# Transposing q and k of batches 4 to 7 with DMA crossbar transposes, loaded two batches ahead

## The chip, the cores and the metric

The kernel runs on one core of one Trainium2 chip. The metric is the time of one execution on the device in microseconds (us). Before the change the median of 14 runs is 361.16 us (360.59 to 365.67).

## What is computed

Eight batches of windowed attention with eight global positions, then a two-layer MLP with a snake activation over all 4608 tokens:

```python
scores = scale * np.matmul(q, k.transpose(0, 1, 3, 2))   # q, k, v: (8, 8, 576, 64), float32
mask = np.abs(pos[:, None] - pos[None, :]) <= 32
mask = mask | is_global[:, None] | is_global[None, :]    # 8 global positions
scores = np.where(mask, scores, -1000000000.0)
...                                                      # softmax over the last axis
x = attn_out.transpose(0, 2, 1, 3).reshape(4608, 512)
h = x @ w_in                                             # 512 -> 2048
s = np.sin(alpha * h)
g = h + s * s / (alpha + 1e-09)
out = g @ w_out                                          # 2048 -> 512
```

## The kernel before

The engines' names in the profile are PE (TensorE, the matmuls), ACT (ScalarE), DVE (VectorE), POOL (GpSimd) and SP (SyncE, which here only issues DMAs). Each engine runs its own instructions strictly in the order in which the program emits them, and waits in place for what an instruction needs.

**Stages.** The loop over `p` has nine stages. Stage p < 8 is the attention of batch p, interleaved with the second matmul of the MLP (`mm2`, L703) of token chunk p − 1, and then the first matmul of the MLP (`mm1`, L664) of chunk p with its activation. A chunk has 512 tokens, a batch 576. Stage 8 has MLP work only. The order within an attention is written out by hand: `attention(p, psA, at)` returns nine parts, steps j = −3 to 5, and after each part `run` emits some slots of `mm2` (`fill`) as further work for PE. A step j finishes unit j (`stage_V`), takes the denominator of unit j + 1 (`stage_D`), masks unit j + 2 (`stage_M`), runs what `at[j]` lists, and starts the scores of unit j + 3 (`stage_Q`). There are six units to a batch; each covers eight of the 48 (head pair, block of 48 query rows) pairs.

**Operands of the scores.** For each of the four head pairs hp, `kTw[hp]` holds the transposed keys in twelve overlapping windows of 112 rows, and `qT[hp]` the transposed queries; both also hold eight columns for the global positions. They are filled for batch p + 1 during the attention of batch p. `stage_T(b, hp)` does that with PE: `T_K` transposes K's 96-row pieces into the PSUM tile `Kps` (12 instructions, L456) and DVE copies the windows to `kTw` (L465); `T_Q` does the same for Q into the PSUM tile `qp`, and ACT copies that to `qT` (L643, after the scores of the step). For p > 1 the four head pairs stand at steps 2 to 5.

**Loads.** K, Q and V come from HBM in float32 and are converted to bfloat16 by DMAs that POOL issues. K and Q of a batch lie in the tiles `KS` and `QS` (pool `qkp`, two buffers each) with the sequence split into six pieces of 96 rows; `load_slots(b)` loads them in halves of the heads (`QUADS`: K, Q, K, Q; 288 KB each as stored, in runs of 64 elements, L128), then V in two halves and a small tail (L109, L115). In the attention of batch p these are the loads of batch p + 1, right after the first parts. `gather_kq(i)` (L259) fetches the global rows of K and Q for the batches 2i and 2i + 1. `globals_in` copies the columns of the global positions (L444, L448, on POOL).

**V.** `shift_v` (L143, L144) makes a second, shifted copy of V's windows from SBUF to SBUF, and `global_v` (L152) spreads the global rows of V; both are DMAs on SP's queue. SP's queue also carries the stores of the results from the tile `osb` (L715, two buffers).

**The end of an attention.** After the last unit, `stage_G` computes the rows of the global queries on DVE (`gs`, `xg`), and POOL writes them into `xT` with eight small copies (L588). `mm1` reads `xT`.

Of the kernel before, what the change touches and what calls it, by code (L numbers as in the profile page):

```python
# [17 lines left out]
def kernel(  # L18
# [11 lines left out]
    nc = tc.nc  # L30
    P = 128
    BF = DT.bfloat16
    F32 = DT.float32

    B, H, S, D = q.shape
# [3 lines left out]
    WIN = 32  # L39
# [4 lines left out]
    NHP = H // 2  # L44
    QB = 48
    KB = QB + 2 * WIN
    NW = S // QB
# [3 lines left out]
    TW = 96  # L51
    NTW = S // TW
# [7 lines left out]
    qkp = ctx.enter_context(tc.tile_pool(name="qkp", bufs=2))  # L60
# [16 lines left out]
    kTw = [const.tile([P, NW, P], BF, name=f"kTw{i}") for i in range(NHP)]  # L77
    qT = [const.tile([P, NW, QC], BF, name=f"qT{i}") for i in range(NHP)]
# [14 lines left out]
    qk = {}  # L93
# [8 lines left out]
    def v_loads(b, cuts):  # L102
        W = VW[b % 2]

        def even(h0, nh):
            Wf = W[:, 0, h0 : h0 + nh].rearrange("p h u d -> p (h u) d")
            n = nh * NU
            if b or h0:
                nc.gpsimd.dma_start(out=Wf[0:KB], in_=heads_ap(v, b, h0, -WIN, KB, 0, n))  # L109
            else:  # L110
                nc.gpsimd.dma_start(out=Wf[WIN:KB], in_=heads_ap(v, b, 0, 0, KB - WIN, 0, n))
                nc.gpsimd.dma_start(out=Wf[0:WIN, 1:n], in_=heads_ap(v, b, 0, -WIN, WIN, 1, n - 1))

        def tail():
            nc.gpsimd.dma_start(  # L115
                out=W[64 : KB - WIN, 1, :, NU - 1, :],
                in_=v[b, :, S - KB + WIN + 64 : S, :].rearrange("h p d -> p h d"),
            )

        return [partial(even, h0, nh) for h0, nh in cuts] + [tail]  # L120

    def kq_loads(b, cuts):
        QS = qkp.tile([TW, H, NTW, D], BF, name="QS")
        KS = qkp.tile([TW, H, NTW, D], BF, name="KS")
        qk[b] = (QS, KS)

        def rows(src, dst, h0, nh):
            nc.gpsimd.dma_start(  # L128
                out=dst[:, h0 : h0 + nh].rearrange("p h t d -> p (h t) d"),
                in_=heads_ap(src, b, h0, 0, TW, 0, nh * NTW),  # L130
            )

        return [partial(rows, s_, d_, h0, nh) for h0, nh in cuts for s_, d_ in ((k, KS), (q, QS))]
# [4 lines left out]
    def load_slots(b):  # L138
        return kq_loads(b, QUADS) + v_loads(b, QUADS)
# [18 lines left out]
    def w_load(dst, src):  # L158
# [23 lines left out]
        out=gall[:],  # L182
        in_=bass.AP(tensor=global_idx.tensor, offset=global_idx.offset, ap=[[0, P], [1, NG]]),
# [34 lines left out]
    def zero_v(i, eng=nc.vector):  # L218
# [5 lines left out]
        out=I8[:, 0:1], in0=I8[:, 0:1], scalar1=3, scalar2=None, op0=ALU.arith_shift_right  # L224
    )
    nc.vector.tensor_scalar(
        out=I8[:, 3:], in0=I8[:, 3:], scalar1=NG - 1, scalar2=None, op0=ALU.bitwise_and
    )
    nc.vector.tensor_scalar(
        out=I8[:, 1:2], in0=I8[:, 0:1], scalar1=2 * NHP, scalar2=None, op0=ALU.bitwise_and  # L230
    )
    nc.vector.tensor_scalar(
        out=identb[:], in0=Af[:], scalar1=0.0, scalar2=None, op0=ALU.is_equal
# [5 lines left out]
        out=Gsel[:, 1:2], in0=I8[:, 0:1], scalar1=2.0, scalar2=None, op0=ALU.mult  # L239
    )  # L240
    nc.vector.scalar_tensor_tensor(
        out=Gsel[:, 2:3], in0=I8[:, 1:2], scalar=1.0 / (2 * NHP) - 2.0, in1=Gsel[:, 1:2],
# [3 lines left out]
        out=Gsel[:, 3:], in0=I8[:, 3:], scalar=0.0, in1=Gf[:], op0=ALU.is_equal, op1=ALU.mult  # L246
    )
    nc.vector.tensor_reduce(
        out=Gsel[:, 0:1], in_=Gsel[:, 3:], axis=mybir.AxisListType.X, op=ALU.add
# [3 lines left out]
        out=rowi[:], in0=Gsel[:, 2:3], scalar=float(S), in1=Gsel[:, 0:1],  # L253
# [19 lines left out]
    def edges(t_):  # L273
# [13 lines left out]
        out=RF[:, 0:1], in0=Af[:, 0:1], scalar1=float(KB + NG - 1), scalar2=None, op0=ALU.is_le  # L287
    )
    nc.vector.scalar_tensor_tensor(
        out=RF[:, 1:2], in0=Af[:, 0:1], scalar=float(KB), in1=RF[:, 0:1],  # L290
# [3 lines left out]
        out=RF[:, 3:], in0=Af[:, 0:NG], scalar1=float(KB + 1), scalar2=None, op0=ALU.is_ge  # L294
    )
    nc.vector.tensor_tensor(
        out=OH[:], in0=T6[:, :, None].to_broadcast([P, NTW, NG]),
# [7 lines left out]
        out=EDGE[:, 0:1], in0=Af[:, 0:1], scalar1=float(WIN), scalar2=None, op0=ALU.is_ge  # L305
    )
    nc.vector.tensor_scalar(
        out=EDGE[:, 2:3], in0=Af[:, 0:1], scalar1=float(WIN + QB - 1), scalar2=None, op0=ALU.is_le
    )
    nc.vector.tensor_tensor(  # L310
        out=EDGE[:, 1:2], in0=EDGE[:, 0:1], in1=EDGE[:, 2:3], op=ALU.mult
    )
    nc.vector.tensor_scalar(
        out=MB[:, 0], in0=Af[:, 0:QB], scalar1=0.0, scalar2=None, op0=ALU.is_ge
    )
    nc.vector.scalar_tensor_tensor(
        out=MB[:, 1], in0=Af[:, 0:QB], scalar=float(2 * WIN), in1=MB[:, 0],
# [155 lines left out]
    def T_Q(b, hp, qpool, qtag, copy):  # L473
        Qps = qpool.tile([P, S], BF, name=qtag)
        T_half(qk[b][0], b, hp, Qps)
        return partial(copy, out=qT[hp][:, :, 0:QB], in_=Qps[:].rearrange("p (i c) -> p i c", c=QB))

    def stage_T(b, hp, pool, tag):
        T_K(b, hp, Kps, nc.vector.tensor_copy)
        return T_Q(b, hp, pool, tag, nc.scalar.copy)  # L480
# [267 lines left out]
    def with_extra(parts, extra, start, per):  # L748
        for i in range(start, len(parts)):
            k_ = (i - start) * per  # L750
            if extra[k_ : k_ + per]:
                parts[i] = partial(chain, parts[i], *extra[k_ : k_ + per])
        return extra[(len(parts) - start) * per :] if len(parts) > start else extra
# [58 lines left out]
    for p in range(NCH):  # L812
        fill = []
        if p == 0:
            phase_0()
            first.close()
        elif p < B:
            with phase_pool("psA", 1) as psA:
                for tag, shape, dt_ in (
                    ("den", [P, NB, QC], F32), ("Sp", [P, 2, CH], F32), ("num", [P, NB, QC], F32),  # L820
                    ("o2", [P, DM], F32), ("qp", [P, S], BF),
                ):
                    psA.tile(shape, dt_, name=tag)
                fill = mm2(p - 1, H2[p - 1], ((psC, "ops"), (psA, "o2")) * 2)
                if p == 1:
                    fill[:8] = [fill[i] for i in (0, 1, 4, 5, 2, 6, 3, 7)]
                T_ = lambda b, hp: partial(stage_T, b, hp, psA, "qp")
                if p == 1:
                    at = {-2: [T_(1, 2)], -1: [T_(1, 3)], 5: [T_(2, 0)]}
                elif p + 1 < B:  # L830
                    at = {2 + hp: [T_(p + 1, hp)] for hp in range(NHP)}
                else:
                    at = {}
                parts = attention(p, psA, at)
                counts = [1, 1, 1, 1, 1, 1, 2, 2, 4]
                fill.pop(0)()
                fill.pop(0)()
                if p + 1 < B:
                    with_extra(parts, load_slots(p + 1), 0, 4)
                    if p < 3:  # L840
                        parts[4] = partial(chain, parts[4], partial(gather_kq, p + 1))
                    for hp in range(NHP):
                        i_ = hp + LEAD + 1
                        parts[i_] = partial(chain, parts[i_], partial(globals_in, p + 1, hp))
                run(parts, counts, fill)
        else:
            fill = mm2(p - 1, H2[p - 1], ((psC, "ops"),) * 4)
        if p == 0:
            setup.release()
            spool = ctx.enter_context(tc.tile_pool(name="spool", bufs=4))  # L850
            osbp = ctx.enter_context(tc.tile_pool(name="osbp", bufs=2))
        with phase_pool("psB", 6) as psB:
            if p > 1:
                H2[p] = hpool.tile([P, NT, CH], BF, name="H2b")
            m1 = mm1(p, H2[p], psB, sq_last if p == B else sq_first if p == 0 else sq_late)
            if p < 3:
                m1[5] = partial(chain, m1[5], partial(globals_t, p + 1, psC, "ops"))
            if p + 1 < B:
                vs = [partial(shift_v, p + 1), partial(global_v, p + 1)]
                ts = {}  # L860
                if p == 0:
                    m1[5] = partial(chain, m1[5], *vs)
                    m1[6] = partial(chain, m1[6], w_loads[3])
                    ts = {12: (1, 0), 14: (1, 1)}
                else:
                    m1[10] = partial(chain, m1[10], *vs)
                    if p == 1:
                        ts = {2: (2, 1), 5: (2, 2), 8: (2, 3)}
                for i_, (b_, hp) in ts.items():
                    m1[i_] = partial(chain, m1[i_], partial(both, stage_T, b_, hp, psC, "ops"))  # L870
            run(m1, [1, 1, 1, 0] * (NT // 4) if p == B else [0] * NT, fill if p == B else [])
            if p == NCH - 1:
                for s in mm2(p, H2[p], ((psB, "hb"), (psC, "ops"), (psB, "hb"), (psB, "hb"), (psC, "ops")), cut=True):
                    s()
# [30 lines left out]
```

The softmax here doesn't subtract the row's maximum and nothing guards it: scores larger than these inputs give would overflow.

## Time and profile before

| | |
|---|---|
| median of 14 runs | 361.16 us (360.59 to 365.67) |
| the profiled execution | 361.23 us, of which the span from first to last instruction is 359.3 us |
| busy share of the span | PE 95%, ACT 68%, DVE 66%, POOL 57% |
| mean granted clock of PE | 0.962 |
| PE's share of the chain that ended last | 64% |
| DMA queue of POOL (software queue) | 123120 packets, 20.04 MB |

The profile shows one execution. Times in it are microseconds from the start of the span unless a column says ns. A line of a timeline or group names the source line, the engine, the operation, output and inputs, and the shapes; "x12" counts instructions; "[0.54 <-ACT qT L643]" is idle time of that engine before the instruction and what ended it. "issue" stands for a wait with no releaser that the profile shows. The chain that ended last follows the work back from the last instruction. Packets overlap on the 16 DMA engines, so that the DMA share can be over 1.

### The profile page before, as it was taken

To read this page: it belongs to the slowest core of one execution; us is meant where nothing else is said; L and a number is where in the kernel's file an instruction comes from. 1 tells how busy PE (TensorE), PEld (TensorE's weight loads), DVE (VectorE), ACT (ScalarE), POOL (GpSimd) and SP (SyncE) were. 2 spreads that over 40 slices of the span, in tenths; PEclk is the share of its full clock that TensorE was granted. 3 is DMA by queue.
4 is the path that set the end of the run, shared out by engine and by line. 5 is a ranking of instruction groups with operands and counts; after the bars stand their busy time and mean duration, and the time that the engine had idled before them with its cause. 6 is when DMAs were issued, how large, how long until landed. Compare 5 with 4: busy or idle time off the path is not lost.

```text
span 359.3 us, 9407 instructions
## 1 busy us (share of the span) xinstructions
PE 340.1 (95%) x3738; PEld 173.1 (48%) x3738; DVE 237.7 (66%) x527; ACT 245.8 (68%) x376; POOL 205.3 (57%) x302
## 2 busy tenths in 40 slices
PE   5589998899999999999999999999999999999996
PEld 5464445454445445544554445444544444444444
DVE  5666695648776687758774878487848864865610
ACT  3656786757886688758874888488858884844401
POOL 9857799245891589158905792479347205755000
PEclk9555999999999999999999999999999999999999
DMA  9999999932399409940994099419932001001012
GB/s 75 168 193 183 202 168 177 178 104 47 20 167 120 111 3 146 149 120 0 138 134 134 10 98 173 111 35 77 184 103 51 30 32 60 0 2 58 30 60 88
DMA packets 133149, 35.39 MB, mean 99 GB/s; under 512 B 121794, under 2 KB 126818, under 8 KB 133106
## 3 DMA queue, kind: packets, MB, share of 16 engines
q0 software_dynamic: 123120, 20.04, 78.1%
q1 hardware_dynamic: 9682, 14.63, 13.7%
q8 instruction: 29, 0.48, 0.5%
q10 hardware_dynamic: 304, 0.14, 0.1%
q14 instruction: 14, 0.11, 0.1%
HBM read 38.95 MB, written 9.44 MB: 135 GB/s over the span
## 4 chain that ended last, share of the span: by engine, by line
PE 64%; ACT 13%; DMA 9%; POOL 4%; DVE 4%; issue 4%; POOLq 1%; ACTq 0%; DVEq 0%
PE hb L664 28%; PE ops L703 12%; PE o L703 12%; DMA w_out<-in_moe_w_out_dram 4%; ACT E L507 3%; PE num L553 3%; PE Sp L501 3%; DMA VW<-in_v_dram 3%; DVE H2b L654 2%; PE den L535 2%; ACT L607 2%; DMA QS<-in_q_dram 2%; PE hb L703 2%; ACT Sb L671 2%; ACT L614 2%
## 5 line engine op out<-in xcount | busy, mean ns | idle before, releaser
L671 ACT ACTIVATE Sb<-hb,alphaT 128x512 bf16<-128x512 f32 x144 | 96.9, 684 | 58.2 <-PE hb L664 54.7
L664 PE MATMUL hb<-xT,w_in 128*128 128x512 bf16 x576 | 129.5, 380 | 0.2 <-DVE H2b L654 0.2
L681 POOL TENSOR_TENSOR S<-Sb 128x512 bf16<-128x512 bf16 x94 | 96.0, 1041 | 48.8 <-ACT Sb L671 45.4
L654 DVE SCALAR_TENSOR_TENSOR H2b<-S,recipT,hb 128x512 bf16<-128x512 bf16 x144 | 102.4, 741 | 30.7 <-POOL S L681 30.3
L664 PEld LDWEIGHTS <-w_in 128*128 128x128 bf16 x576 | 55.8, 98 | 67.3 <-issue 1.2
L703 PEld LDWEIGHTS <-H2b 128*128 128x128 bf16 x560 | 49.7, 98 | 56.2 <-issue 2.3
L703 PE MATMUL ops<-w_out,H2b 128*128 128x512 bf16 x304 | 73.9, 380 | 0.9 <-DMA w_out<-in_moe_w_out_dram 0.9
L703 PE MATMUL o<-w_out,H2b 128*128 128x512 bf16 x224 | 54.4, 381 | 0.0
L588 POOL COPY xT<-xg 128x4 bf16 x64 | 12.9, 201 | 67.9 <-DVE xg L586 64.4
L507 ACT ACTIVATE E<-Sp 128x896 bf16<-128x896 f32 x48 | 43.5, 906 | 8.5 <-PE Sp L501 5.2
L572 DVE TENSOR_TENSOR xT<-num,rec 128x384 bf16<-128x384 f32 (+1 forms) x60 | 26.0, 454 | 23.6 <-PE num L553 15.5
L541 ACT ACTIVATE lnd<-den 128x384 f32<-128x384 f32 x48 | 23.7, 493 | 18.8 <-PE den L535 18.2
L513 DVE TENSOR_TENSOR E<-E,MASK 128x896 bf16<-128x896 bf16 x48 | 30.1, 627 | 7.3 <-ACT E L507 7.3
L501 PE MATMUL Sp<-qT,kTw 64*128 64x56 bf16 x768 | 19.9, 189 | 8.0 <-ACT E L507 2.8
L553 PEld LDWEIGHTS <-VW 120*64 120x64 bf16 (+1 forms) x768 | 17.3, 117 | 19.6 <-issue 11.3
L543 ACT ACTIVATE rec<-lnd 128x384 f32<-128x384 f32 x48 | 25.1, 524 | 1.5
L501 PEld LDWEIGHTS <-kTw 64*128 64x128 bf16 x768 | 15.5, 96 | 19.7 <-issue 13.8
L465 DVE COPY kTw<-Kps 128x1344 bf16<-128x1344 bf16 x29 | 24.4, 840 | 0.0
L681 DVE TENSOR_TENSOR S<-Sb 128x512 bf16<-128x512 bf16 x34 | 17.6, 517 | 9.0 <-ACT Sb L671 8.9
L553 PE MATMUL num<-E,VW 120*64 120x56 bf16 (+1 forms) x720 | 20.6, 198 | 0.7 <-issue 0.7
L128 POOL DMA_DIRECT2D KS<-in_k_dram x18 | 20.7, 1150 | 0.6 <-issue 0.6
L535 PE MATMUL den<-E,ones 120*64 120x448 bf16 x96 | 18.9, 387 | 1.5 <-issue 0.8
(133 smaller groups left out, 308.2 us busy)
## 6 DMA issues: line engine op xcount, KB each, us to landing
out_dram<-osb SPq DMA_DIRECT2D x35, 256.0 KB
KS<-in_k_dram POOLq DMA_DIRECT2D x14, 288.0 KB
QS<-in_q_dram POOLq DMA_DIRECT2D x14, 288.0 KB, 17.2
VW<-in_v_dram POOLq DMA_DIRECT2D x12, 336.0 KB, 11.3
VW<-VW SPq DMA_DIRECT2D x7, 384.0 KB
w_in<-in_moe_w_in_dram POOLq DMA_DIRECT2D x2, 1024.0 KB
w_out<-in_moe_w_out_dram POOLq DMA_DIRECT2D x2, 1024.0 KB
VW<-VW SPq DMA_DIRECT2D x7, 240.0 KB
```

The lines of the kernel that those rows point to most:

```text
L501: nc.tensor.matmul(out=Sp[:, t, m * QC : (m + 1) * QC], lhsT=kTw[hp][pr, i, :], rhs=qT[hp][pr, i, :], start=True, stop=True, skip_group_ch ...
L507: nc.scalar.activation(out=E[:], in_=Sp[:, :, 0:EW], func=AF.Exp, scale=scale)
L513: nc.vector.tensor_tensor(out=E[:], in0=E[:], in1=mk[:, None, :].to_broadcast([P, 2, EW]), op=ALU.mult)
L535: nc.tensor.matmul(out=den[pr].rearrange("p u c -> p (u c)"), lhsT=ones[0 : KB + NG], rhs=E[0 : KB + NG, t, :], start=True, stop=True, ski ...
L543: nc.scalar.activation(out=rec[:], in_=lnd[:], func=AF.Exp, scale=-1.0)
L553: nc.tensor.matmul(out=num[pr, m, :], lhsT=W[0:nk, i % 2, 2 * hp + t, i // 2, :], rhs=E[0:nk, t, m * QC : (m + 1) * QC], start=b > 0 or m ...
L572: nc.vector.tensor_tensor(out=xT[:, hp, x0 : x0 + nb * QB].rearrange("p (u c) -> p u c", u=nb), in0=num[:, m0 : m0 + nb, 0:QB], in1=rec[:, ...
L654: nc.vector.scalar_tensor_tensor(out=H2b[:, n_, :], in0=s_[:], scalar=recipT[:, n_ : n_ + 1], in1=h_, op0=ALU.mult, op1=ALU.add,)
L664: nc.tensor.matmul(out=h2[:], lhsT=w_in[:, ci, nt * P : (nt + 1) * P], rhs=xT[:, ci, c * CH : (c + 1) * CH], start=(ci == 0), stop=(ci == ...
L671: nc.scalar.activation(out=Sb[:], in_=h2[:], func=AF.Sin, scale=alphaT[:, nt : nt + 1])
L681: eng.tensor_tensor(out=S2[:], in0=Sb[:], in1=Sb[:], op=ALU.mult)
L703: nc.tensor.matmul(out=ops[:], lhsT=H2b[:, nt, ts * P : (ts + 1) * P], rhs=w_out[:, nt, :], start=(nt == 0), stop=(nt == NT - 1),)
```

## The change

For the batches 4 to 7 PE's transposes are replaced. `x_loads(b)` loads K and Q two batches ahead, in the attention of batch b − 2, one DMA for each 96-row piece over all heads (twelve DMAs of 96 KB, again issued by POOL), so that a row holds all heads side by side. In the `mm1` stage of p = b − 2, `cross` issues one crossbar transpose (`dma_start_transpose`) for each piece on SP's queue, into a tile `XT[0]` (K) or `XT[1]` (Q) from the same pool as `KS` and `QS`. In the attention of batch b − 1, at the steps where `stage_T` stood, `stage_X` copies from these SBUF tiles: three DVE copies to `kTw`, one ACT copy to `qT`.

Around it: the attention of p = 2 first issues `gather_kq(3)`, then batch 3's K and Q each in one DMA over all heads (instead of halves), V in one DMA, V's tail, and the row loads of batch 4; batch 3 is still transposed by PE there. For p = 3 to 6 only V of batch p + 1 is loaded in the attention of p, and K and Q of batch p + 2 where there is one. The value shift and broadcast of SP move from slot 10 of `mm1` to slot 0 for p > 1, and the crossbar transposes follow in slots 1 to 12.

```diff
+    def x_loads(b):
+        QS = qkp.tile([TW, NTW, H, D], BF, name="QS")
+        KS = qkp.tile([TW, NTW, H, D], BF, name="KS")
+        qk[b] = (QS, KS)
+
+        def rows(src, dst, jt):
+            nc.gpsimd.dma_start(
+                out=dst[:, jt],
+                in_=bass.AP(
+                    tensor=src.tensor, offset=src.offset + (b * H * S + jt * TW) * D,
+                    ap=[[D, TW], [S * D, H], [1, D]],
+                ),
+            )
+
+        return [partial(rows, s_, d_, jt) for s_, d_ in ((k, KS), (q, QS)) for jt in range(NTW)]
+
+    def cross(b, kq, jt):
+        if jt == 0:
+            XT[kq] = qkp.tile([P, NHP, S], BF, name=("KS", "QS")[kq])
+        src = qk[b][1 - kq]
+        nc.sync.dma_start_transpose(
+            out=XT[kq][:, :, jt * TW : (jt + 1) * TW],
+            in_=src[:, jt].rearrange("p h d -> p (h d)"),
+        )
+
+    def stage_X(b, hp):
+        kx, qx = XT[0][:, hp], XT[1][:, hp]
...
+        nc.vector.tensor_copy(out=kTw[hp][:, 1 : NW - 1, 0:KB], in_=win(1, NW - 2))
+        nc.vector.tensor_copy(out=kTw[hp][:, 0, WIN:KB], in_=kx[:, 0 : KB - WIN])
+        nc.vector.tensor_copy(out=kTw[hp][:, NW - 1, 0 : KB - WIN], in_=kx[:, S - KB + WIN : S])
+        return partial(
+            nc.scalar.copy, out=qT[hp][:, :, 0:QB], in_=qx.rearrange("p (i c) -> p i c", c=QB)
+        )
...
-                    at = {2 + hp: [T_(p + 1, hp)] for hp in range(NHP)}
+                    at = {2 + hp: [partial(stage_X, p + 1, hp) if p > 2 else T_(p + 1, hp)] for hp in range(NHP)}
...
-                    with_extra(parts, load_slots(p + 1), 0, 4)
-                    if p < 3:
-                        parts[4] = partial(chain, parts[4], partial(gather_kq, p + 1))
+                    if p == 1:
+                        with_extra(parts, load_slots(2), 0, 4)
+                        parts[4] = partial(chain, parts[4], partial(gather_kq, 2))
+                    else:
+                        WHOLE = ((0, H),)
+                        ld = v_loads(p + 1, WHOLE)
+                        if p == 2:
+                            ld = [partial(gather_kq, 3)] + kq_loads(3, WHOLE) + ld
+                        xl = x_loads(p + 2) if p + 2 < B else []
+                        with_extra(parts, ld + xl[:NTW], 0, 4)
+                        with_extra(parts, xl[NTW:], 5 if p == 2 else 3, 3)
...
-                    m1[10] = partial(chain, m1[10], *vs)
+                    i_ = 10 if p == 1 else 0
+                    m1[i_] = partial(chain, m1[i_], *vs)
+                    if p > 1 and p + 2 < B:
+                        for i in range(2 * NTW):
+                            m1[1 + i] = partial(chain, m1[1 + i], partial(cross, p + 2, i // NTW, i % NTW))
```

More of the change, by code (lines that the diff above doesn't have):

```diff
@@ L476, in T_Q @@
         return partial(copy, out=qT[hp][:, :, 0:QB], in_=Qps[:].rearrange("p (i c) -> p i c", c=QB))
+    XT = {}
+    def x_loads(b):
[21 more added lines that the diff above has]
+        kx, qx = XT[0][:, hp], XT[1][:, hp]
+        base = kx[:, 0:1]
+        win = lambda i0, n: bass.AP(
+            tensor=base.tensor, offset=base.offset + i0 * QB - WIN,
+            ap=[list(base.ap[0]), [QB, n], [1, KB]],
+        )
[4 more added lines that the diff above has]
+            nc.scalar.copy, out=qT[hp][:, :, 0:QB], in_=qx.rearrange("p (i c) -> p i c", c=QB)
+        )
     def stage_T(b, hp, pool, tag):
```

## The prediction

> **What bounds the kernel now.** I read the page first, then the chain of waits in order of time, then the timelines of single engines in two batches. The page has TensorE (PE) busy nearly throughout and, from the fifth slice on, at the full granted clock:
>
> ```profile
> PE 340.1 (95%) x3738; PEld 173.1 (48%) x3738; DVE 237.7 (66%) x527; ACT 245.8 (68%) x376; POOL 205.3 (57%) x302
> ...
> PEclk9555999999999999999999999999999999999999
> ```
>
> The chain in order of time shows where each batch's first MLP product (`hb`, L664) begins:
>
> ```profile
> 117.83 5.18 PE hb L664 x24
> ...
> 154.84 13.83 PE hb L664 x64
> ...
> 192.39 13.83 PE hb L664 x64
> ...
> 229.09 13.83 PE hb L664 x64
> ...
> 265.79 13.83 PE hb L664 x64
> ...
> 300.21 4.33 PE hb L664 x20
> ```
>
> These are p = 2 to 7. The differences are the periods of p = 3 to 7: 37.01, 37.55, 36.70, 36.70 and 34.42. The last is the control that the trace hands us: p = 7 has the same attention and fill, but no batch after it, so no transposes, no kTw and qT copies and no loads. It is 2.28 shorter than p = 5 and 6. In p = 5 the PE timeline has the 24 transposes of one head pair (12 into Kps, 12 into qp, L456) four times; from the first to what follows them they take 0.61, 0.65, 0.61 and 0.91, together 2.78. So nearly all of their time is on PE's path; p = 7 gives 0.5 back in small waits for ACT and DVE.
>
> For the loads I need p = 2, where the change does something else: the POOL timeline (issues), the PE timeline (first use) and the table of stretches (us, busy time and count of PE, PEld, DVE, ACT, POOL, PE clock, DMA share, GB/s):
>
> ```profile
> 95.16 1.27 POOL L128 DMA_DIRECT2D KS<-in_k_dram  x1
> 96.42 1.21 POOL L128 DMA_DIRECT2D QS<-in_q_dram  x1
> ...
> 99.94 2.57 POOL L109 DMA_DIRECT2D VW<-in_v_dram  x2
> ...
> 103.33 1.17 POOL L259 DMA_INDIRECT GKQ<-in_k_dram,rowi  x1 [0.30 <-issue]
> 104.80 0.98 POOL L259 DMA_INDIRECT GKQ<-in_q_dram,rowi  x1 [0.30 <-issue]
> ```
>
> ```profile
> 103.94 0.42 PE L456 MATMUL Kps<-identb,KS 96*64 96x96 bf16 x12
> 104.47 0.45 PE L456 MATMUL qp<-identb,QS 96*64 96x96 bf16 x12
> ```
>
> ```profile
> 97.00:98.00 1.00, 1.00 (x14) 0.32 (x5) 0.35 (x1) 0.84 (x1) 1.00 (x2) 1.00 1.20 77
> 98.00:102.00 4.00, 3.90 (x79) 2.08 (x78) 2.85 (x7) 3.57 (x7) 4.00 (x4) 1.00 2.17 142
> 102.00:104.00 2.00, 2.00 (x50) 1.03 (x44) 1.42 (x5) 1.80 (x4) 1.70 (x3) 1.00 1.92 222
> 104.00:108.00 4.00, 3.22 (x81) 1.95 (x79) 2.90 (x7) 2.77 (x6) 3.36 (x10) 1.00 2.44 158
> ```
>
> Data starts about 2 us after the first issue (95.16 to about 97.1) and then moves at no more than 158 GB/s. Quarter loads are 288 KB each (half the heads of K or Q). The first two, 590 kB, are in by about 102, 2 us before the transposes need them at 103.94.
>
> **What is removed, p = 3 to 6.** No T in these four attentions: PE loses 2.78 per batch, of which the control says 2.28 is gained. But the control also lacks the copies, which stay. By form:
>
> ```profile
> L465 DVE COPY kTw<-Kps 128x1344 bf16<-128x1344 bf16 x29 | 24.4, 840 | 0.0
> L643 ACT COPY qT<-qp 128x576 bf16<-128x576 bf16 x23 | 14.6, 633 | 0.3
> ```
>
> ACT: the qT copy from SBUF; the nearest row is the square of 512 elements from SBUF (L679), 0.630, so about 0.69 instead of 0.63, four per batch. In p = 7 ACT is the pacer only up to the last exponent at 291.0; after it PE has the fill products, and lnd at 294.49 still waits 1.14 for PE. Two more copies there are covered nearly whole. DVE: one copy from PSUM becomes three from SBUF, 1120, 80 and 80 elements. The small ones cost like the 128-element copy of L430, 0.216; the big one lies between that and 0.84. So 0.65 to 1.27 a pair, I take 0.9, near the 0.84 removed. Where does it show? The third pair's copies stand in DVE's queue ahead of the last xT product (L572), which heads the tail xT, gn, gs, xg, eight POOL copies (L588, 2.03), `hb`. In p = 7 that product waits 0.90 for PE, and POOL ends at 300.0 against PE's 300.2. With the copies ahead of it the tail ends some 0.3 late. So 2.28 − 0.3 = 2.0 a batch, **8.0** for four. Ends: 1.4 a batch if the copies cost 1.27, 2.6 with all of PE's 2.78 gained and p = 4's extra 0.85 (a PE stall with no releaser, "issue", at 181.3) gone too; 5.6 to 10.4.
>
> **What is added, p = 2.** Batch 3 is still transposed by PE in p = 2, at steps 2 to 5, but its loads change: both gathers go first, then all heads of K in one DMA, then all of Q. Gathers: 103.33 minus the gap to 105.78 is 2.75, so K is issued at about 97.9 instead of 95.16, data from about 100.2 (a longer issue may make it later). The whole K and Q are 1180 kB. By the same stretches: 1.8 us at 142, then 2 us at about 91 (102 to 104 has a 262 kB store in its 222) bring 440 kB, and 158 after that the other 740 kB in 4.7. K ends at about 105, Q at 108.7, and half a microsecond to a whole one passes until it is seen. The first transpose of K waits from 103.9 to about 105.7, the first of Q until about 109.4 instead of 104.47. PE runs in order; behind it stand Sp of the last unit, the fill and every later product, and ACT and DVE run dry after it. **Cost 4.9**, ends 3.5 (landing as fast as data, some waits after 104.84, such as the 0.54 for qT at 107.35, caught up) and 6.5 (K's long issue delays its first data).
>
> The clock: since 37 us it has been full, and the longest PE wait there is 0.9, so no row shows what an idle stretch of 3.7 does. Before 37 it was 0.50 with PE busy 3.94 of 4 us (32 to 36), so recovery can take 5 us of work, up to 2.5 lost; I take 0.4. The Trainium skill, "TensorE: Matmul & The Clock Gate", Part 1, says that one idle window of about 3.4 us halves the clock until another such window is busy; by it this term would be up to 1.7, an estimate from that page that no row here shows.
>
> **What is moved or hidden.** POOL: twelve row loads of 96 KB (768 runs) cost between the 0.535 of L115 (256 runs) and the 0.88 of the pair loads (1152), I take 0.75: 9.0 against 4 × 1.18, less 0.5 from one V load (2.07) for two. That is 3.8 more per batch; POOL waits 7 to 9 for xg (L588) there. In p = 2 it is 18 in all, ending near 114, with the globals' copies behind it (2.2), before xg. The bytes of p = 3 to 5 are those of before; p = 2 carries 5/3, 3080 kB or about 21 us at 150, done by 123; the crosses there can start no sooner anyway. Shift and broadcast move from slot 10 to 0 of the MLP, but on SP's queue nothing stands between:
>
> ```profile
> 156.09 0.55 SPq L143 DMA_DIRECT2D VW<-VW  x1
> 156.70 0.66 SPq L144 DMA_DIRECT2D VW<-VW  x1
> 157.40 1.63 SPq L152 DMA_DIRECT2D VW<-VgX  x2
> ```
>
> They already follow the last store at once; this costs nothing. Then come twelve crossbar transposes per batch. Counted from the start of `hb` (154.84), SP is free at +4.2; the first kTw copy needs K's six at about +25 (180.37), the first qT copy Q's at +26.1 (180.92), SP's next store comes at +19 (osb has two buffers, the third is filled at +33). So 12 c + 1 must fit in 22: c under **1.75**. No row shows a crossbar transpose. The nearest are these SBUF copies: 0.55 at the low end, and one at a time, each landed before the next (about 1.7 after its issue), 2.3. I take 1.0, near the copies as they are queued: hidden. The Trainium skill speaks against the change here: "VectorE: DVE Perf Modes", The three transpose paths, gives 1309 ns for a 128×128 transpose through the crossbar against 390 on TensorE and prefers TensorE where PSUM will do. Paid singly for the 48 blocks of a batch that would be 63 us, 42 too late four times, and the kernel would take some 525 us, an estimate from that page that no row here shows.
>
> **Sum.** 361.23 (span 359.3 and 1.9 around it; the median is 361.16, so no correction) − 8.0 + 4.9 + 0.4 = **358.5**.
>
> **Rivals.** (1) Slower: the crosses come late. Place: DVE's kTw copies and ACT's qT copies at step 2 of p = 3 to 6, both in order. Price: 12 × 4 × (c − 1.75). At c = 1.81 the net gain is gone; at 2.3 it is +26, 385. For: no such row, and twelve in series. Against: copies of 240 to 384 KB issue in 0.6. Chance 0.15. (2) The copies pace attention instead of PE: only 1 a batch is gained, 358.5 + 4 = 362.5. For: ACT is nearly gapless up to the last exponent; against: p = 7's 1.14 of slack. Chance 0.13; with it goes a p = 2 stall of 8, which also gives about 361.5. (3) No stall in p = 2, because K and Q of batch 3 land in time: 353.2. Against: 1180 kB at 158 GB/s. Chance 0.10. (4) Mine, 0.62, own range 355.5 to 361.
>
> **How the numbers follow.** 0.3% (1.1 us, about what a measurement of this kernel tells from no change) draws the lines at 360.1 and 362.2. Mine gives 0.51 faster, 0.08 same, 0.03 slower; (3) 0.10 faster; (2) 0.04 same, 0.09 slower; (1) 0.15 slower. The range takes mine, half of (3), (2), and the mild part of (1): 353 to 366.
>
> **What would show it.** In p = 2 a PE wait for QS of 3 to 5 us near 105 to 110; `hb` of p = 2 at about 123; periods of p = 3 to 6 near 34.7 without L456; kTw copies near 0.9 a pair with no DMA ahead of them; twelve transposes on SP ending before +20. A wait of DVE or ACT for them, periods near 36, or no wait for QS would make it wrong.

## The result and the profile after

The changed kernel takes **364.83 us** (median of 10 runs, 363.55 to 366.93), against 361.31 for the kernel before (47 runs): ratio **1.010, interval 1.008 to 1.012**. It is slower by 3.5 us, where 358.5 and "faster" were forecast. The profiled execution took 365.33 (span 363.6), 4.10 more than the profiled one of before.

The page after, busy time and granted clock:

```profile
PE 332.1 (91%) x3354; PEld 164.1 (45%) x3354; DVE 235.0 (65%) x559; ACT 246.3 (68%) x376; POOL 218.4 (60%) x327
...
PEclk9558999999996999999999999899999999999999
```

PE is busy 8.0 us less: 384 transposes are gone, at 2.78 a batch 11.1 in all, and the stretches at half clock below give some 3.5 of that back (an estimate from the table's clock). POOL is busy 13.1 more. PE's clock now dips in two places, in the slices that begin at 109 and 227 us. The chain in order of time gives the starts of `hb` for p = 2 to 7 again (now L705):

```profile
124.68 5.18 PE hb L705 x24
...
160.70 4.49 PE hb L705 x20
...
196.68 4.49 PE hb L705 x20
...
233.44 15.67 PE hb L705 x64
...
269.88 13.99 PE hb L705 x64
...
304.45 4.35 PE hb L705 x20
```

The first and last rows start 0.15 after the group that the PE timeline shows (before, all six do, by 0.15 to 0.17). Taken from the PE timeline for every kernel, the period that ends with the first `hb` of p is, in us:

| kernel | p=1 | p=2 | p=3 | p=4 | p=5 | p=6 | p=7 | p=3 to 6 |
|---|---|---|---|---|---|---|---|---|
| before | 40.79 | 40.95 | 37.01 | 37.55 | 36.70 | 36.70 | 34.43 | 147.96 |
| after | 39.28 | 48.71 | 36.18 | 35.97 | 36.76 | 36.44 | 34.44 | 145.35 |

The 4.25 by which p = 7 begins later is +0.61 up to the first `hb` of p = 0, −1.51 in p = 1 (whose code is the same in both; among the kernels below that share it, it varies from 39.2 to 41.7), **+7.76 in p = 2** and **−2.61 in p = 3 to 6**. Forecast were +5.3 and −8.0. Both terms have to be explained, the second above all.

**p = 2**, PE timeline and the table of stretches (us, busy time and count of PE, PEld, DVE, ACT, POOL, PE clock, DMA share, GB/s):

```profile
103.74 0.36 PE L576 MATMUL den<-E,ones 120*64 120x448 bf16 x2
106.60 0.45 PE L456 MATMUL Kps<-identb,KS 96*64 96x96 bf16 x12 [2.50 <-DMA KS<-in_k_dram]
110.68 0.69 PE L456 MATMUL qp<-identb,QS 96*64 96x96 bf16 x12 [3.64 <-DMA QS<-in_q_dram]
```

```profile
107.00:111.00 4.00, 0.36 (x11) 0.32 (x10) 0.86 (x1) 0.00 (x0) 2.25 (x4) 0.60 2.73 155
111.00:115.00 4.00, 4.00 (x72) 2.22 (x68) 0.65 (x2) 2.37 (x4) 1.47 (x4) 0.55 2.43 158
```

PE stands still for K and for Q, 6.14 together. Then the clock is half: a mean of 0.60 over 4 us and 0.55 over the next 4 are 3.2 and 3.6 us at 0.50. In the second stretch PE is busy throughout, so the 3.6 there cost 1.8. Waits and clock make 7.9, against the 7.76 measured.

**p = 3 to 5**, POOL timeline ahead of `hb` of p = 5, first one row of before, then of after in two answers; then the PE timeline, and the rows of PE's and of POOL's waits (total, times, longest):

```profile
226.03 2.04 POOL L588 COPY xT<-xg 128x4 bf16 x8 [7.69 <-DVE xg L586]
```

```profile
212.14 2.03 POOL L109 DMA_DIRECT2D VW<-in_v_dram  x1
214.16 0.54 POOL L115 DMA_DIRECT2D VW<-in_v_dram  x1
214.69 4.59 POOL L486 DMA_DIRECT2D KS<-in_k_dram  x6
```

```profile
224.70 4.80 POOL L486 DMA_DIRECT2D QS<-in_q_dram  x6 [5.42 <-DMA VW<-in_v_dram]
229.49 0.40 POOL L444 COPY kTw<-GT 128x96 bf16<-128x96 bf16 x1
...
231.35 2.04 POOL L629 COPY xT<-xg 128x4 bf16 x8
```

```profile
233.44 8.75 PE L705 MATMUL hb<-xT,w_in 128*128 128x512 bf16 x32 [2.04 <-POOL xT L629]
```

```profile
PE hb L705 <- POOL xT L629: 5.5, 4, 2.0
```

```profile
POOL QS L486 <- DMA VW<-in_v_dram: 12.4, 3, 5.4
...
POOL QS L486 <- DMA QS<-QS: 4.4, 1, 4.4
```

Before, POOL idled 7.69 ahead of the same xT copies and began them at 226.03, when xg was there. Now it idles 5.42 **ahead of Q's first row load**, because that waits for V's load, which is no data of its own; the row loads, the globals' copies and the xT copies stand behind it in POOL's queue and run without a gap. DVE is through with xg at 229.10, 2.25 before POOL begins to copy it. `hb` waits 0.84, 1.25 and 2.04 in p = 3, 4 and 5 (the fourth wait, 1.41, is in p = 0). After the 2.04 the clock is half once more:

```profile
234.00:235.00 1.00, 1.00 (x5) 0.36 (x3) 0.00 (x0) 0.26 (x1) 0.00 (x0) 0.54 0.89 190
235.00:236.00 1.00, 1.00 (x4) 0.38 (x3) 0.00 (x0) 0.43 (x1) 0.49 (x1) 0.50 0.82 209
236.00:237.00 1.00, 1.00 (x3) 0.30 (x2) 0.42 (x1) 0.49 (x1) 0.55 (x1) 0.50 1.03 223
237.00:238.00 1.00, 1.00 (x5) 0.43 (x4) 0.33 (x1) 0.23 (x2) 0.72 (x1) 0.75 0.84 101
```

That is 3.4 us at 0.50, 1.7 lost: the 15.67 in place of 13.99 for the 64 `hb` products in the chain above, and the 36.44 of p = 6, in which nothing is loaded any more for K and Q.

Why does a Q row load wait for V? The order of issue fits one reading at each of these places: a POOL load waits until the load issued eight before it has landed. V, its tail, K's six rows, Q's first: V is the eighth before. In p = 2 the row load behind K, Q, V, tail and five rows waits 1.75 for the whole Q (eight before is Q), the next one 2.53 for V (POOL timeline of p = 2):

```profile
110.92 0.77 POOL L486 DMA_DIRECT2D KS<-in_k_dram  x1 [1.75 <-DMA QS<-in_q_dram]
...
114.69 2.30 POOL L486 DMA_DIRECT2D QS<-in_q_dram  x3 [2.53 <-DMA VW<-in_v_dram]
```

The kernel before issued seven to nine loads a batch, so that the eighth before was nearly always a load of the batch before, long landed.

**The parts that came as forecast.** SP timeline of p = 3, where `hb` began at 160.70, and the copies by form:

```profile
163.90 7.73 SPq L500 DMA_TRANSPOSE KS<-KS  x6
171.73 7.71 SPq L500 DMA_TRANSPOSE QS<-QS  x6
```

```profile
L684 ACT COPY qT<-QS 128x576 bf16<-128x576 bf16 x16 | 10.7, 666 | 0.3 <-DMA QS<-QS 0.2
L512 DVE COPY kTw<-KS 128x1120 bf16<-128x1120 bf16 x16 | 7.9, 492 | 0.0
...
L514 DVE COPY kTw<-KS 128x80 bf16<-128x80 bf16 x16 | 4.3, 270 | 0.0
L513 DVE COPY kTw<-KS 128x80 bf16<-128x80 bf16 x16 | 4.3, 268 | 0.0
```

A crossbar transpose takes 1.29 of SP's queue here (7.73 / 6), 1.28 to 1.43 over the four batches, under the 1.75 allowed, and the queue is through with the last one 18.7 after `hb` began (17.6 to 20.7 over the four). The kTw copies take 1.03 a pair, the qT copy 0.67, and they wait for next to nothing.

### The profile page after: what moved, and what is told of

It is laid out like the page before. It is cut to its first block, busy times and chain, and to the rows that moved or that the text cites. A ratio compares the mean times of both kernels' runs of the same rounds, so it can differ in the third digit from the quotient of the medians.

```text
span 363.6 us, 8825 instructions
## 1 busy us (share of the span) xinstructions
PE 332.1 (91%) x3354; PEld 164.1 (45%) x3354; DVE 235.0 (65%) x559; ACT 246.3 (68%) x376; POOL 218.4 (60%) x327
## 4 chain that ended last, share of the span: by engine, by line
PE 43%; DMA 18%; POOL 16%; issue 9%; ACT 6%; DVE 4%; SPq 2%; POOLq 1%; ACTq 0%; DVEq 0%
PE hb L705 21%; PE ops L744 9%; DMA VW<-in_v_dram 6%; PE o L744 6%; DMA QS<-in_q_dram 5%; POOL S L722 4%; DMA w_out<-in_moe_w_out_dram 4%; POOL QS L486 4%; DVE H2b L695 3%; DMA QS<-QS 2%; PE hb L744 2%; ACT E L548 2%; POOL xT L629 2%; ACT Sb L712 2%; SPq L500 2%
## 5 line engine op out<-in xcount | busy, mean ns | idle before, releaser
L705 PE MATMUL hb<-xT,w_in 128*128 128x512 bf16 x576 | 130.6, 383 | 5.7 <-POOL xT L629 5.5
L722 POOL TENSOR_TENSOR S<-Sb 128x512 bf16<-128x512 bf16 x94 | 96.5, 1045 | 46.4 <-ACT Sb L712 41.9
L705 PEld LDWEIGHTS <-w_in 128*128 128x128 bf16 x576 | 56.2, 99 | 74.3 <-issue 9.3
L744 PE MATMUL o<-w_out,H2b 128*128 128x512 bf16 x224 | 55.3, 385 | 0.0
L629 POOL COPY xT<-xg 128x4 bf16 x64 | 13.1, 205 | 37.4 <-DVE xg L627 34.0
L486 POOL DMA_DIRECT2D QS<-in_q_dram x24 | 19.0, 801 | 16.9 <-DMA VW<-in_v_dram 12.4
L542 PEld LDWEIGHTS <-kTw 64*128 64x128 bf16 x768 | 16.1, 96 | 20.7 <-issue 15.6
L722 DVE TENSOR_TENSOR S<-Sb 128x512 bf16<-128x512 bf16 x34 | 17.6, 517 | 10.3 <-ACT Sb L712 10.2
L486 POOL DMA_DIRECT2D KS<-in_k_dram x24 | 18.5, 780 | 4.1 <-issue 2.4
## 6 DMA issues: line engine op xcount, KB each, us to landing
VW<-in_v_dram POOLq DMA_DIRECT2D x6, 672.0 KB, 12.3
```

Source lines behind the costliest of these rows:

```text
L486: nc.gpsimd.dma_start(out=dst[:, jt], in_=bass.AP(tensor=src.tensor, offset=src.offset + (b * H * S + jt * TW) * D, ap=[[D, TW], [S * D, H ...
L542: nc.tensor.matmul(out=Sp[:, t, m * QC : (m + 1) * QC], lhsT=kTw[hp][pr, i, :], rhs=qT[hp][pr, i, :], start=True, stop=True, skip_group_ch ...
L705: nc.tensor.matmul(out=h2[:], lhsT=w_in[:, ci, nt * P : (nt + 1) * P], rhs=xT[:, ci, c * CH : (c + 1) * CH], start=(ci == 0), stop=(ci == ...
L722: eng.tensor_tensor(out=S2[:], in0=Sb[:], in1=Sb[:], op=ALU.mult)
L744: nc.tensor.matmul(out=ops[:], lhsT=H2b[:, nt, ts * P : (ts + 1) * P], rhs=w_out[:, nt, :], start=(nt == 0), stop=(nt == NT - 1),)
```

## The experiments

My theory after the traces: the 8 us are there, and are given back in two places, the late K and Q of batch 3 and POOL's waits. The rival is that the new copies and transposes eat the gain. Ratios are to the kernel before, run on the same chip.

**Only p = 2's loads, in the kernel before** (`before_whole`). No crossbar, no row loads.

```diff
-                    with_extra(parts, load_slots(p + 1), 0, 4)
-                    if p < 3:
+                    if p == 2:
+                        WHOLE = ((0, H),)
+                        with_extra(parts, [partial(gather_kq, 3)] + kq_loads(3, WHOLE) + v_loads(3, WHOLE), 0, 4)
+                    else:
+                        with_extra(parts, load_slots(p + 1), 0, 4)
+                    if p < 2:
```

> The kernel before, with one part of the change alone: in p = 2 both gathers first, then batch 3's K, Q and V each in one DMA over all heads. Theory (whole loads land too late for the transposes of batch 3, PE waits about 6 and then works at half clock for some 4): hb of p = 2 starts about 7.8 later than in the kernel before, 361.3 + 7.8 = 369. Rival (the stall of p = 2 comes from the row loads of batch 4 that share the queue and the DMA engines): no or little stall without them, 361 to 363.

369.83, ratio 1.023 (1.018 to 1.027). The PE timeline has the same two waits at the same place, and the period of p = 2 is 49.03:

```profile
106.96 0.45 PE L456 MATMUL Kps<-identb,KS 96*64 96x96 bf16 x12 [2.15 <-DMA KS<-in_k_dram]
111.06 0.69 PE L456 MATMUL qp<-identb,QS 96*64 96x96 bf16 x12 [3.66 <-DMA QS<-in_q_dram]
```

So gathers first and whole loads alone cost 8 us, clock included; neither the crossbar nor the row loads are needed for it.

**Batch 3 in halves, in the kernel after** (`after_halves`), gathers behind as before.

```diff
-                            ld = [partial(gather_kq, 3)] + kq_loads(3, WHOLE) + ld
+                            ld = load_slots(3)
+                            parts[4] = partial(chain, parts[4], partial(gather_kq, 3))
```

> The changed kernel, with batch 3 loaded as in the kernel before (K and Q in halves of the heads, V in two, the gathers at part 4), the row loads of batch 4 behind it. Theory: no PE wait for KS or QS in p = 2, no half clock there, hb of p = 2 near 117, 364.8 - 7.8 = 357. Rival (the delay only moves: batch 4's rows land later, its crossbar transposes and with them p = 3 come late): 361 or more, with a DVE or ACT wait for the transposes in p = 3.

364.57, ratio 1.008 (1.005 to 1.011): a miss by 7.6. The rival's time came, but not its place. PE no longer waits for K and Q at L456, yet the period of p = 2 is 47.35. The wait moved to the end of the same attention (PE timeline, then POOL timeline):

```profile
123.39 1.01 PE L705 MATMUL hb<-xT,w_in 128*128 128x512 bf16 x2 [7.54 <-POOL xT L629]
```

```profile
105.80 0.78 POOL L486 DMA_DIRECT2D KS<-in_k_dram  x1 [1.09 <-DMA KS<-in_k_dram]
107.60 0.77 POOL L486 DMA_DIRECT2D KS<-in_k_dram  x1 [1.02 <-DMA QS<-in_q_dram]
109.71 0.77 POOL L486 DMA_DIRECT2D KS<-in_k_dram  x1 [1.33 <-DMA VW<-in_v_dram]
112.59 1.04 POOL L259 DMA_INDIRECT GKQ<-in_k_dram,rowi  x1 [2.11 <-DMA VW<-in_v_dram]
```

Issue order here is K, Q, K, Q, V, V, tail, six K rows, gather: the fourth, fifth and sixth row and the gather each wait for the load eight before. POOL held up p = 2 all along, hidden behind PE's own waits for K and Q: two causes, one behind the other. It also shows how my expectation went wrong a second time, by the same step: POOL's waits were left out.

**K's rows ahead of V in p = 3 to 5** (`after_vlast`). The load eight before Q's first row is then a K row.

```diff
-                        with_extra(parts, ld + xl[:NTW], 0, 4)
+                        with_extra(parts, ld + xl[:NTW] if p == 2 else xl[:NTW] + ld, 0, 4)
```

> The changed kernel, for p of 3 and more with the order K rows, V, tail, Q rows on POOL instead of V, tail, K rows, Q rows. The program lets a POOL DMA start only when the one eight before it has landed; now the first Q row load has a K row load eight before it and not V. Theory (POOL is held by that rule, and its late copies into xT hold hb): POOL's wait before the Q rows ends at the landing of the Q transposes, 4 to 5 sooner in p = 4 and 5, not sooner in p = 3; PE's wait for xT L629 falls from 5.5 to about 1 and the half clock in p = 5 goes; 364.8 - 4 = 361, 2 either way. Rival (the wait is for the crossbar transposes that still read QS): the same waits, 364.8.

361.20, ratio 0.999 (0.997 to 1.002): 3.6 less than the kernel after, for an edit that changes nothing but the order of two groups of loads. POOL's wait for V stays once (2.7, in p = 2); what remains in p = 3 to 5 is another one, for the tile: Q's rows overwrite a buffer that the last batch's transposes still read.

```profile
POOL QS L486 <- DMA QS<-QS: 9.2, 3, 4.8
...
POOL QS L486 <- DMA VW<-in_v_dram: 2.7, 1, 2.7
```

Periods of p = 3 to 6: 35.17, 34.76, 36.25, 34.75. The 4.8 is in p = 5, where POOL again starts its xT copies late, at 229.90.

**PE kept busy in p = 2** (`after_warm`), 26 products of no use around the first T.

```diff
+                if p == 2:
+                    def hot(n):
+                        wp = psA.tile([P, NB, QC], F32, name="num")
+                        for _ in range(n):
+                            nc.tensor.matmul(...)
+                    def T_hot():
+                        hot(10)
+                        T_K(3, 0, Kps, nc.vector.tensor_copy)
+                        hot(16)
+                        return T_Q(3, 0, psA, "qp", nc.scalar.copy)
+                    at[2] = [T_hot]
```

> The changed kernel, with 10 products of 448 columns that nothing reads ahead of the first K transposes of batch 3 in p = 2, and 16 ahead of the first Q transposes. The loads are as late as before; PE is busy instead of idle. Theory (about 2 of the 7.8 lost in p = 2 is the half clock): the granted clock stays 1.00 from 107 to 115, hb of p = 2 about 1.9 sooner, 363. Rival (the clock costs nothing, the wait all): 364.8 or, with the products behind the landing, up to 1 more.

The clock stayed at 1.00 and the period of p = 2 fell from 48.71 to 47.11:

```profile
107.00:111.00 4.00, 3.63 (x29) 1.79 (x28) 0.86 (x1) 0.00 (x0) 2.30 (x3) 1.00 3.28 155
```

The kernel's median did not fall: 365.04, ratio 1.010 (1.007 to 1.013); the profiled execution, with 362.33, was the lowest of six. So the 1.6 in p = 2 rests on one trace, and for the whole time the run is inconclusive.

**No K and Q of batches 5 to 7** (`after_noloads`).

```diff
-                        xl = x_loads(p + 2) if p + 2 < B else []
+                        xl = x_loads(p + 2) if p == 2 else []
...
-                    if p > 1 and p + 2 < B:
+                    if p == 2:
                         for i in range(2 * NTW):
```

> Leaves out K and Q of batches 5 to 7: their row loads and crossbar transposes are not made, and the attention steps of p = 3 to 6 all copy batch 4's transposed tiles (so the copies of DVE and ACT stay, V stays). Theory (what p = 3 to 5 still lose is POOL held by the waits of its row loads, which makes the xT copies and so hb late): no hb waits for xT after p = 2, the periods of p = 3 to 6 are 34.6 to 34.9 instead of 36.2, 36.0, 36.8 and 36.4, in sum 6.5 less, and the kernel takes about 358.5. Rival (the SBUF copies of kTw and qT pace attention, as the prediction's second rival had it): they are all still there, the periods stay near 36 and the kernel near 364.5. The period of p = 2 stays near 48.5 by both.

Periods of p = 3 to 6: **35.02, 34.73, 34.73, 34.72**, with all the copies of kTw and qT in place; so they pace nothing, and the rival falls. The median, 361.29, ratio 0.999 (0.997 to 1.001), is 2.8 above the 358.5 expected: p = 2 took 49.89 here, with 10.2 us at half clock, and the start-up varies.

**K's rows first, Q's rows behind the globals** (`after_qlate`), p = 3 to 5.

```diff
-                        with_extra(parts, ld + xl[:NTW], 0, 4)
-                        with_extra(parts, xl[NTW:], 5 if p == 2 else 3, 3)
+                        with_extra(parts, ld + xl[:NTW] if p == 2 else xl[:NTW] + ld, 0, 4)
+                        if p == 2:
+                            with_extra(parts, xl[NTW:], 5, 3)
                     for hp in range(NHP):
                         ...
+                    if p > 2 and xl:
+                        parts[7] = partial(chain, parts[7], *xl[NTW:])
```

> For p = 3 to 5 the six K row loads go ahead of V, and the six Q row loads behind the copies of the globals instead of ahead of them; p = 2 is unchanged. Theory (only the waits of the row loads hurt, not their 9 us of issue): Q's rows then wait for nothing and fit in the 7 to 9 us in which POOL idles before xg; periods of p = 3 to 6 near 34.8, kernel 358.5 to 359.5. Rival (the issue time itself is too much for POOL): xT copies end late by some 1 to 2 as before, and the kernel stays at 361, where the kernel with only V moved behind K's rows was.

The same periods as without the loads, to 0.01: 35.02, 34.73, 34.73, 34.72, though all loads are made. POOL timeline of p = 5:

```profile
211.55 4.62 POOL L486 DMA_DIRECT2D KS<-in_k_dram  x6
216.16 1.98 POOL L109 DMA_DIRECT2D VW<-in_v_dram  x1
...
221.89 4.59 POOL L486 DMA_DIRECT2D QS<-in_q_dram  x6
228.58 2.19 POOL L629 COPY xT<-xg 128x4 bf16 x8 [2.10 <-DVE xg L627]
```

No row load waits, and POOL has 2.10 to spare before xg. V, issued at 216.16, landed only some 8.6 after its issue, so Q's first rows went out while V was still in flight: the wait in the kernel after was not for V's data, but for its place in the order. Counted from the `hb` of p = 4, the xT copies of p = 5 begin at 32.5, against 34.7 in the kernel after. The 9.2 us of issue were hidden; the waits were not. Kernel: 360.49, ratio 0.999 (0.996 to 1.002), 1 to 2 above the expectation; in its profile p = 1 took 41.71 (with 3.4 us at half clock at 65), against 39.28 in that of the kernel after.

**Only p = 2 mended** (`after_p2`): halves first, batch 3's gathers in p = 1, Q's rows of batch 4 behind the xT copies.

```diff
                         parts[4] = partial(chain, parts[4], partial(gather_kq, 2))
+                        parts[6] = partial(chain, parts[6], partial(gather_kq, 3))
...
-                            ld = [partial(gather_kq, 3)] + kq_loads(3, WHOLE) + ld
+                            ld = load_slots(3)
...
-                        with_extra(parts, xl[NTW:], 5 if p == 2 else 3, 3)
+                        if p > 2:
+                            with_extra(parts, xl[NTW:], 3, 3)
...
+                    if p == 2:
+                        parts[8] = partial(chain, parts[8], *xl[NTW : NTW + 3])
...
+                    if p == 2:
+                        for i_, f in zip((3, 5, 6), xl[NTW + 3 :]):
+                            m1[i_] = partial(chain, m1[i_], f)
```

> Only p = 2 is changed: batch 3 is loaded in halves first, as in the kernel before; its gathers move to p = 1, behind those of batch 2; three of batch 4's Q row loads go behind the xT copies and three into the first MLP steps. Theory (p = 2 has two causes one behind the other: K and Q of batch 3 landing late, and, with that gone, POOL held by 15 loads ahead of the xT copies): both are gone, the period of p = 2 falls from 48.7 to 41 to 42.5, the clock stays up, kernel about 358. Rival (18 us of POOL work or 3 MB in one batch is too much wherever it stands): the wait only moves again, to the MLP's squares or the crossbar transposes, period 46 or more, kernel 362 to 364.5.

357.55, ratio **0.988** (0.984 to 0.992). The period of p = 2 is 39.65, below that of before, and the clock stays up. p = 3 and 5 are worse (38.21 and 38.32), with POOL's longest waits at 6.9 for the transposes and 4.6 for V.

**Both** (`after_best`): the edits of the last two together.

> Both edits together: p = 2 with halves first, early gathers and late Q rows; p = 3 to 5 with K rows, V, globals, then Q rows. Theory: the two losses are independent, so the periods are about 41.5 for p = 2 and 34.8 for p = 3 to 6: 365 less 7 less 6.5, about 352, which is 9 under the kernel before. Rival (a third limit, the clock or the copies, takes over): 356 or more.

**352.95**, ratio **0.978** (0.974 to 0.982), 8.5 under the kernel before, with the change's purpose kept whole. The chain:

```profile
152.56 13.99 PE hb L705 x64
...
222.07 13.99 PE hb L705 x64
...
256.95 13.99 PE hb L705 x64
...
291.54 4.35 PE hb L705 x20
```

Periods of p = 2 to 6: 39.65, 36.96, 34.75, 34.76, 34.88. Most of the 2 us in p = 3 is one wait: `hb` waits 1.77 for H2b at 129.90. Just before it, at 126.62, a square on DVE (L722) takes 2.56 us, where the mean in the kernel after is 0.52, while POOL works off four squares in a row that stand behind Q's late rows. `after_p2` has the same pair. That the late rows are the cause fits this, but no run tests it.

## Why the prediction was wrong

- **The gain was right, and is shown.** 2.0 a batch was forecast, from the control p = 7 less 0.3 for the copies. With POOL's waits gone (`after_qlate`), p = 3 to 6 take 139.20, 8.76 less than before: 1.97 to 1.99 in p = 3, 5 and 6, and 2.82 in p = 4, whose extra 0.85, which the prediction kept for the end of its range, went too. Against p = 7's 34.42 the periods stay 0.3 long (0.6 in p = 3), near what was put down for the copies. That it is the copies is not shown: `after_noloads` rules out the loads of K and Q, but V's loads and the globals' copies are left beside them. The crossbar's c, SP's time for one transpose, was 1.28 to 1.43 for the 1.0 taken; rival 1 needed 1.75. Rival 2, copies that pace, is refuted by `after_noloads`; rival 3, no stall, by the trace.
- **The step that failed** is "What is moved or hidden", POOL: "That is 3.8 more per batch; POOL waits 7 to 9 for xg (L588) there." It put POOL at nothing in the sum. The issues were counted and sized nearly right (0.75 taken, 0.78 to 0.80 measured). What was not asked is whether the queue can issue them at that moment. Q's first row load waited for V, the load eight before it (4.49 and 5.42 in p = 4 and 5), or for the transposes that still read its buffer (4.44 in p = 3). With the 3.8 this is 8.2 to 9.2, more than the cover: that was 7.7 in p = 5 before, and xg comes 1.3 sooner now. Cost in p = 3 to 6: 145.35 − 139.20 = **6.2**, of which 1.7 is the half clock that followed one wait of 2.04. The prediction's own sign of being wrong, "periods near 36", came, but for these waits and not for the copies.
- **p = 2: place and mechanism right, size short.** Forecast 4.9 for the waits, measured 6.1 (K used at 106.60, not 105.7; Q at 110.68, not 109.4). K was issued at 96.74, sooner than the 97.9 forecast, but used 9.9 later where 7.8 was forecast: what ran long is the load, not the gathers. The clock was put at 0.4 and cost 1.8 by the table of stretches; `after_warm` gives 1.6. The estimate of up to 1.7 from the Trainium skill's "TensorE: Matmul & The Clock Gate", Part 1, is near this, but no bound: in `after_noloads` p = 2 has 10.2 us at half clock, with PE busy in 6 of them from 111 to 117, 3 lost. And the page's condition, a whole idle window of about 3.4 us, is not what p = 5 shows, where 2.04 us of idle were followed by 3.4 at half clock. The prediction's "the longest PE wait there is 0.9" is also a misreading: the kernel before has a PE wait of 1.33 for ACT at 64.43, with the clock at 1.00.
- And "In p = 2 it is 18 in all, ending near 114" is the same step once more: POOL's waits were left out, and POOL was through with the last Q row load at 119.70. It cost nothing as long as PE waited for K and Q, and 7.5 once it did not (`after_halves`, whose gathers also stand behind the K rows). The two together are the largest lesson in size: with the loads' order mended alone p = 2 took 47.35, with POOL's mended too (`after_p2`, the gathers in p = 1) 39.65.
- The sum with the measured terms: 361.23 − 8.8 + 6.2 + 7.8 − 0.9 (start and p = 1, unchanged code) = 365.5, against 365.33. The terms are differences of the periods, so this says only that no stretch was left out.
- That 364.83 lies within 353 to 366 is luck: the range reached up there for late crossbar transposes, and these were in time.
- The Trainium skill's "VectorE: DVE Perf Modes", The three transpose paths, speaks of 1309 ns for a 128×128 block through the crossbar. Here one transpose of 96 × 512, four blocks of 96 × 128, took 1.28 to 1.43 us of SP's queue, so that price paid for each block is not what this case shows.

## What to carry to other kernels

When loads are added to a queue, write its order out and ask of each load what it must wait for before it can be issued: the load some places ahead of it in the same queue, and the last reader of its buffer. A price for the issue alone is no price. Put loads whose data are needed last behind the small copies that the bound engine needs next. And when a wait is removed and the time stays, look for a second queue that was late at the same place.

## What was not expected of the hardware

- POOL's loads wait for the load issued eight before: eight waits of two kernels, in p = 2, 4 and 5, fit it, 1.0 to 5.4 us each (in p = 3 the wait of 4.44 was for the transposes that read the buffer); moving V behind K's rows removes the wait for V in p = 4 and 5, and leaves 2.05 and 4.80 for the transposes. In p = 2 of the kernel after there is one idle stretch of POOL more, 2.38 at 106.86 with no releaser in the trace, which this reading doesn't explain. It stays open, as does whether the rule is the chip's or the program's: the expectation of `after_vlast` took it for the program's.
- A PE wait of 2.04 us was followed by 3.4 us at half clock, one of 3.64 (after 2.50 and 0.45 of work) by 6.8, while with 26 products in the same gap the clock stayed at 1.00 (one trace). The length of the wait alone doesn't decide it: in p = 1 one of 1.34 in `after_qlate` was followed by 3.4 us at half clock, while one of 1.33 at the same place in the kernel before, one of 1.74 there in `after_p2` and one of 1.64 in p = 4 of `after_halves` left it at 1.00. What decides is open.
- V's load takes 12.3 us (median, from the page's DMA issues) to land with six row loads behind it, and 10.3 where the row loads of three batches are left out.
